# DeltaNet followed by a maxout feed-forward: block products in sets of 32 on 64 rows, weights fetched from ScalarE's queue, TensorE in program order through the first group

## The chip, the cores and the metric

One core of a Trainium2 chip. The metric is the device time of one execution in us. Every kernel was also run in rounds beside the kernel before on the same chip; ratios below come from such rounds. Times within an execution (landmarks, stages, waits) come from one profiled execution of each kernel. Engines: PE is TensorE (PEld its weight loads), DVE VectorE, ACT ScalarE, POOL GpSimd, SP SyncE.

## The reference, cut to what matters

```python
# q, k, v: (4, 8, 768, 48), beta: (4, 8, 768)
k_n = k / (norm(k) + 1e-6)
for t in range(768):
    y[t]  = q[t] @ state
    v_old = k_n[t] @ state
    state = state + beta[t] * outer(k_n[t], v[t] - v_old)
x = y as (3072 tokens, 384)
h = maximum(maximum(x @ w1, x @ w2), x @ w3)      # w1, w2, w3: 384 x 768
out = h @ w_out                                   # 768 x 384
```

## The kernel before

The sequence is cut into 12 chunks of 64 tokens. A chunk needs the inverse of a triangular 64x64 matrix for each of 32 (batch, head) pairs. It is built from smaller blocks: VectorE solves the diagonal blocks row by row (`solve`), and TensorE joins them. For the first two groups (chunks 0 to 3) VectorE solves blocks of 16, joined to 32 (`halves_z`, `halves_u`, tiles p_e and p_f, called e and f below) and then to 64 (`join_z`, `join_u`, tiles p_z and p_j: z and j); for later groups it solves blocks of 32. With the inverse `ut`, the chain of a chunk goes on: `new` (p_u), `step` (p_s, the state), `to_y` (p_y), `to_x` (p_x, transposed for the feed-forward). `ffn(m)` then runs the maxout layer of 512 tokens (p_h, p_o). The attention work of group m+1 is spread between the maxout items of group m; only group 0 has nothing to hide behind. That opening, and group 0's maxout, are what the change rearranges.

```python
    def fetch():                       # one weight piece, 384 KB
        ...
            st = work.tile([128, 2 * 384], U32, name="w_bits", bufs=4)
            nc.sync.dma_start(out=..., in_=src)

    TILES = [(bb, g) for bb in range(2) for g in range(2)]
    # rows(bb): 64 rows, half bb;  block(bb, f): 32 rows, half f of half bb

    def halves_z(c):                   # e: 64 products of 32 rows, 16 columns
        ...
        for g in range(2):
            for h in range(H):
                for bb in range(2):
                    for f in range(2):
                        r = block(bb, f)
                        nc.tensor.matmul(p_v[r, g, h],
                            at[g][r, h, BL * f : BL * (f + 1)], d[r, g, h, HB:])

    def new(c):                        # u, for comparison
        for h in range(H):
            for bb, g in TILES:
                nc.tensor.matmul(p_v[rows(bb ^ g), g, h],
                    ut[c % NU][rows(bb), g, h], rhs[rows(bb), g, h])

    # the opening, all engines in program order:
    ...; halves_z(0); halves_u(0); halves_z(1); join_z(0); ...; halves_u(1)
    join_u(0); ...; join_z(1); ...; new(0); ...; join_u(1); ...; to_y(0); to_x(0)
    # then ffn(0), ordered by the scheduler, with the links of chunks 1 to 3 between
```

A product in float32 is two instructions (two passes), each with its weight load; so a set of 32 products is 64 TensorE instructions in the tables.

## Time and profile before

| | |
|---|---|
| time before, first three runs | 615.88 us median |
| TensorE idle until the first p_h (76.1 us), between there and 160, after 160 | 32.5, 14.7, 8.2 us |
| clock at half in 43 to 76 | all of it |
| TensorE instructions | 8794 matmuls, as many weight loads |

The views behind this table, and how they are read, stand in the prediction.

### The profile page before, as it was taken

The page shows a single profiled execution, that of the slowest core. Times are in us where ns is not written, and L with a number is a line of the kernel's source. Part 1 is how long each engine was busy: PE and PEld are TensorE (multiplying, and loading weights), DVE is VectorE, ACT ScalarE, POOL GpSimd, SP SyncE. Part 2 cuts the span into 40 slices and gives each one's busy share as a digit, 9 for nine tenths or more (in the row PEclk, how much of TensorE's full clock was granted, in tenths as well). Part 3 has the DMA queues.
Part 4 walks back from the last instruction along what each step waited for, and adds up shares of the span by engine and source line. Part 5 has one row for each costly group of instructions (what it writes and reads, how often), then busy time and mean ns, then how long its engine had stood idle before and what let it go on. Part 6 is the DMA issues. An engine that isn't in the chain of part 4 may idle for free.

```text
span 614.8 us, 19609 instructions
## 1 busy us (share of the span) xinstructions
PE 559.4 (91%) x8794; PEld 342.7 (56%) x8794; DVE 304.8 (50%) x713; ACT 160.8 (26%) x292; POOL 77.4 (13%) x108
## 2 busy tenths in 40 slices
PE   6644667978999999999999999999999999999996
PEld 5534556867655665555655546655556455554443
DVE  1652599328739962389542499432595422101110
ACT  3231545236613142121233121232111111110000
POOL 5360274114400000000000000000000000000000
PEclk9655569897999999999999999999999999999999
DMA  8985257652673254421452321522103100010002
GB/s 156 178 203 123 73 137 141 137 145 70 125 123 65 48 121 74 87 49 31 90 105 58 63 54 27 108 54 61 21 14 82 28 2 3 13 39 1 0 1 52
DMA packets 140820, 45.46 MB, mean 74 GB/s; under 512 B 126400, under 2 KB 136384, under 8 KB 140736
## 3 DMA queue, kind: packets, MB, share of 16 engines
q1 hardware_dynamic: 137744, 41.45, 33.2%
q0 software_dynamic: 880, 2.36, 1.4%
q8 instruction: 69, 1.13, 0.8%
q10 hardware_dynamic: 2112, 0.39, 0.4%
q14 instruction: 15, 0.12, 0.1%
HBM read 29.98 MB, written 14.16 MB: 72 GB/s over the span
## 4 chain that ended last, share of the span: by engine, by line
PE 70%; DVE 16%; issue 5%; POOL 3%; DMA 2%; SPq 2%; ACT 1%; POOLq 0%; ACTq 0%; DVEq 0%
PE p_h L707 37%; PE p_o L731 15%; DVE y_bl L453 4%; DVE tmp L449 4%; PE p_g L356 3%; PE p_t L334 3%; PE p_k L597 2%; DVE h L717 1%; PE p_q L597 1%; PE p_y L660 1%; PE p_z L564 1%; SPq L112 1%; PE p_s L643 1%; PE p_u L625 1%; PE p_e L521 1%
## 5 line engine op out<-in xcount | busy, mean ns | idle before, releaser
L707 PE MATMUL p_h<-xt,w_sb 128*128 128x512 f32 (+1 forms) x702 | 301.3, 575 | 2.0 <-DVE xt L693 1.3
L707 PEld LDWEIGHTS p_h<-xt,w_sb 128*128 128x128 f32 x702 | 130.9, 195 | 124.8 <-issue 116.6
L717 DVE TENSOR_TENSOR h<-h,p_h 128x512 f32<-128x512 f32 (+1 forms) x78 | 50.2, 644 | 142.9 <-PE p_h L707 142.8
L731 PE MATMUL p_o<-wo_sb,h 128*128 128x384 f32 x288 | 97.1, 490 | 2.5 <-DVE h L717 2.4
L731 PEld LDWEIGHTS p_o<-wo_sb,h 128*128 128x128 f32 x288 | 53.3, 190 | 41.3 <-DVE h L717 6.5
L453 DVE TENSOR_TENSOR y_bl<-y_bl,tmp 128x31 f32<-128x31 f32 (+20 forms) x154 | 52.7, 342 | 4.2
L449 DVE TENSOR_TENSOR tmp<-x_bl,y_bl 128x31 f32<-128x31 f32 (+20 forms) x154 | 51.8, 337 | 4.2
L715 ACT COPY h<-p_h 128x512 f32<-128x512 f32 (+1 forms) x39 | 21.5, 551 | 122.1 <-PE p_h L707 122.1
L356 PE MATMUL p_g<-kqt 64*64 64x64 f32 (+1 forms) x1280 | 32.1, 249 | 11.0 <-ACT kqt L340 10.5
L275 POOL TENSOR_TENSOR v_t<-v_t,nrm 128x768 f32<-128x768 f32 x12 | 18.2, 1513 | 180.7 <-DMA v_t<-in_v_dram 93.7
L356 PEld LDWEIGHTS p_g<-kqt 64*64 64x64 f32 x1280 | 27.6, 149 | 18.1 <-ACT kqt L340 14.0
L739 ACT COPY o_sb<-p_o 128x384 f32<-128x384 f32 x24 | 11.5, 480 | 88.3 <-PE p_o L731 85.3
L340 ACT COPY kqt<-p_t 128x512 f32<-128x512 f32 (+1 forms) x32 | 25.2, 797 | 31.2 <-PE p_t L334 31.0
L509 DVE STREAM_TRANSPOSE t<-ut 32x256 f32<-32x256 f32 x32 | 13.9, 434 | 23.1 <-DMA ut<-y_d 22.8
L236 POOL TENSOR_TENSOR w_sb<-mant,up 128x384 int32<-128x384 int32 x18 | 18.7, 1036 | 20.6 <-DVE mant L232 11.6
L334 PE MATMUL p_t<-ident,kpad 128*128 128x128 f32 x96 | 17.0, 308 | 4.3 <-DVE pt L366 2.1
L366 DVE TENSOR_TENSOR pt<-p_g,mask 128x512 f32<-128x512 f32 x24 | 16.1, 686 | 9.1 <-PE p_g L356 8.8
L374 ACT COPY at<-p_g 128x512 f32<-128x512 f32 x20 | 11.6, 586 | 32.2 <-DVE pt L366 29.7
L213 POOL TENSOR_SCALAR mant<-mant 128x384 f32<-128x384 f32 x24 | 12.7, 531 | 51.9 <-ACT mant L209 51.8
L625 PEld LDWEIGHTS p_u<-v_t,ut 64*64 64x64 f32 x768 | 13.2, 142 | 8.9 <-issue 7.7
L334 PEld LDWEIGHTS p_t<-ident,kpad 128*128 128x128 f32 x96 | 12.5, 156 | 8.8 <-issue 5.5
L643 PEld LDWEIGHTS p_s<-u,kpad 64*64 64x64 f32 x704 | 12.2, 144 | 9.1 <-issue 5.3
(97 smaller groups left out, 503.1 us busy)
## 6 DMA issues: line engine op xcount, KB each, us to landing
w_bits<-in_moe_w_dram SPq DMA_DIRECT2D x18, 384.0 KB, 3.6
at_d<-at SPq DMA_DIRECT2D x36, 128.0 KB, 2.5
qpad<-in_q_dram SPq DMA_DIRECT2D x48, 96.0 KB, 3.1
v_t<-in_v_dram SPq DMA_DIRECT2D x24, 192.0 KB, 4.3
out_dram<-o_sb SPq DMA_DIRECT2D x48, 96.0 KB, 2.2
kpad<-in_k_dram SPq DMA_DIRECT2D x44, 96.0 KB, 3.4
x_bl<-at_d SPq DMA_DIRECT2D x22, 128.0 KB, 3.6
y_d<-y_bl SPq DMA_DIRECT2D x11, 256.0 KB, 3.0
```

The lines of the kernel that those rows point to most:

```text
L236: nc.gpsimd.tensor_tensor(out=dst.bitcast(I32), in0=mant_v.bitcast(I32), in1=up_v, op=ALU.add)
L334: nc.tensor.transpose(p_t[:, i, j * 128 : (j + 1) * 128], src[:, 2 * j : 2 * j + 2], ident,)
L340: nc.scalar.copy(kqt.rearrange("p j b i t -> p i (j b) t")[:, some], p_t.rearrange("p i (x t) -> p i x t", t=C)[:, some],)
L356: nc.tensor.matmul(p_g[rows(bb ^ (g * i)), par, c0 : c0 + C * (1 + whole)], kq[:, 0], kq if whole else kq[:, i],)
L449: nc.vector.tensor_tensor(out=t_v, in0=row.to_broadcast(t_v.shape), in1=column.to_broadcast(t_v.shape), op=ALU.mult,)
L453: nc.vector.tensor_tensor(out=rest, in0=rest, in1=t_v, op=ALU.subtract)
L597: nc.tensor.matmul(p_b[rows(bb), par, c0 : c0 + D], kqt[g][rows(par), j, bb ^ g, i], st[rows(par), bb ^ g, g, j],)
L625: nc.tensor.matmul(p_v[rows(bb ^ g), g, h], ut[c % NU][rows(bb), g, h], rhs[rows(bb), g, h],)
L707: nc.tensor.matmul(p_h, w_sb[i][:, t, f * 128 : (f + 1) * 128], xt[:, t, lo : lo + w], start=(t == 0), stop=(t == KT - 1),)
L715: nc.scalar.copy(h, p_h)
L717: nc.vector.tensor_tensor(out=h, in0=h, in1=p_h, op=ALU.max)
L731: nc.tensor.matmul(p_o, hs[f][:, i * 128 : (i + 1) * 128], wo_sb[:, f], start=(f == 0), stop=(f == FT - 1),)
```

## The change

The intent: fewer TensorE instructions and steps before the first p_h; weight fetches that no longer block SyncE's queue; and TensorE's order in group 0 fixed by hand. Its core (left out: the same edits for the links' tables, loads and warm-up):

```diff
-    def fetch():
+    def fetch(queue=nc.scalar):
...
+        for h in range(H):                                  # halves_z
+            for bb, g in TILES:
+                r = rows(bb)
+                nc.tensor.matmul(
+                    p_v[r, g, h], at[g][r, h], second[r, g, h, :, 1]
+                )
+        nc.scalar.copy(zs[c % NU], p_v)
+        fine[c] = [square("t") for g in range(2)]
         for g in range(2):
-            for h in range(H):
-                for bb in range(2):
-                    for f in range(2):
-                        r = block(bb, f)
-                        nc.tensor.matmul(...)
...
+        for h in range(H):                                  # halves_u
+            for bb, g in TILES:
+                r = rows(bb)
+                nc.tensor.matmul(p_v[r, g, h], t[g][r, h], z[r, g, h])
+        (four scaled copies of the corners into ut; the copies of fill() are gone)
...
-        queues = (nc.gpsimd, nc.sync) if m == 0 else one_queue  # end of solve
...
-                    to = dg[cc] if m < FINE else ut[cc][:, :, :, BL * half :]
-                    queues[half].dma_start(
+                    nc.sync.dma_start(          # solved blocks, straight into ut
...
-    load_beta()                                             # the opening
+    load_beta()            # later, and in GpSimd's queue
+    blocks(0, two_queues)  # x_bl: two transfers on SyncE, two on GpSimd
+    sums_0 = first_squares()
...
+    first_norms(*sums_0)
+    for n in range(2):
+        fetch(nc.sync)     # two weight pieces directly behind x_bl
     load_k(6)
...
-    halves_z(1)            # chunk 1 leaves the opening
...
+    FIRST = { 0: "s0 e1 T2", 1: "k1 f1 P2 T3", 2: "z1 P3", 3: "q1 j1", 4: "u1 T4", ...
+    by_hand.enter_context(tc.manual_schedule(engines={mybir.EngineType.PE}))
+    for i, _ in enumerate(ffn(0)):
...
-        nc.gpsimd.memset(y_bl, 0.0)
+        (nc.vector if m else nc.gpsimd).memset(y_bl, 0.0)
```

More of the change, by code (lines that the diff above doesn't have):

```diff
@@ L140, in load_beta @@
             half, cc = divmod(i, 2)
-            nc.sync.dma_start(
+            nc.gpsimd.dma_start(
                 out=beta_bl[32 * i : 32 * (i + 1)],
@@ L161 @@
     ut = [const.tile([128, 2, H, C], FP32, name=f"ut{i}") for i in range(NU)]
-    dg = [const.tile([128, 2, H, BL], FP32, name=f"dg{i}") for i in range(NU)]
     t1 = [const.tile([128, 2, H, BL], FP32, name=f"t1{i}") for i in range(NU)]
@@ L189, in fetch @@
             st = work.tile([128, 2 * 384], U32, name="w_bits", bufs=4)
-            nc.sync.dma_start(
+            queue.dma_start(
                 out=st.rearrange("p (a b) -> p a b", a=a), in_=src
@@ L464, in solve @@
         for cc in range(2):
-            for half in (1, 0):
+            for half in range(2):
                 for bb in range(2):
                     r0 = C * bb + BL * half
-                    to = dg[cc] if m < FINE else ut[cc][:, :, :, BL * half :]
-                    queues[half].dma_start(
-                        out=to[r0 : r0 + BL].rearrange("p g h i -> p (g h) i")[
-                            :, :, 0:BL
-                        ],
+                    nc.sync.dma_start(
+                        out=ut[cc][
+                            r0 : r0 + BL, :, :, BL * half : BL * (half + 1)
+                        ].rearrange("p g h i -> p (g h) i"),
                         in_=y_d[half, cc, 2 * bb : 2 * bb + 2].rearrange(
@@ L498, in block @@
         return slice(C * bb + BL * f, C * bb + BL * f + n)
-    def parts_of(c):
-        if c < 2 * FINE:
-            return [dg[c % NU]] * 2
-        return [ut[c % NU][:, :, :, BL * f : BL * (f + 1)] for f in range(2)]
     def turn_t1(c):
-        first, t = parts_of(c)[0], t1[c % NU]
         for bb, g in TILES:
-            nc.vector.transpose(out=t[block(bb ^ g), g], in_=first[block(bb), g])
+            nc.vector.transpose(
+                out=t1[c % NU][block(bb ^ g), g], in_=ut[c % NU][block(bb), g, :, 0:BL]
+            )
@@ L511, in halves_z @@
+    fine = {}
     def halves_z(c):
         at = [ats[2 * c + g] for g in range(2)]
-        d, t, z = dg[c % NU], t1[c % NU], zs[c % NU]
+        u_t = ut[c % NU]
+        second = u_t.rearrange("p g h (f two x) -> p g h f two x", two=2, x=HB)
         p_e = ps_two("p_e")
-        p_v = by_head(p_e, HB)
-        for g in range(2):
-            for h in range(H):
-                for bb in range(2):
-                    for f in range(2):
-                        r = block(bb, f)
-                        nc.tensor.matmul(
-                            p_v[r, g, h],
-                            at[g][r, h, BL * f : BL * (f + 1)],
-                            d[r, g, h, HB:],
-                        )
@@ L526, in halves_z @@
-        nc.scalar.copy(z[:, :, :, 0:HB], p_v)
-        nc.vector.transpose(
-            out=t.rearrange("p g h x -> p (g h x)"),
-            in_=d.rearrange("p g h x -> p (g h x)"),
-        )
+        p_v = by_head(p_e, BL)
+        for h in range(H):
[3 more added lines that the diff above has]
+                    p_v[r, g, h], at[g][r, h], second[r, g, h, :, 1]
+                )
+        nc.scalar.copy(zs[c % NU], p_v)
+        fine[c] = [square("t") for g in range(2)]
@@ L532, in halves_u @@
+        for g in range(2):
+            nc.vector.transpose(
+                out=fine[c][g].rearrange("p h x -> p (h x)"),
+                in_=u_t[:, g].rearrange("p h x -> p (h x)"),
+            )
     def halves_u(c):
-        d, t, z = dg[c % NU], t1[c % NU], zs[c % NU]
+        t, z = fine.pop(c), zs[c % NU]
         p_f = ps_two("p_f")
-        p_v = by_head(p_f, HB)
-        for g in range(2):
-            for h in range(H):
-                for bb in range(2):
-                    for f in range(2):
-                        r = block(bb, f, HB)
-                        nc.tensor.matmul(
-                            p_v[block(bb, f), g, h], t[r, g, h], z[r, g, h, 0:HB]
-                        )
@@ L544, in halves_u @@
-        corner = d[:, :, :, HB:]
-        nc.vector.tensor_tensor(out=corner, in0=corner, in1=p_v, op=ALU.subtract)
-        turn_t1(c)
-    def fill(c):
-        for bb in range(2):
-            for f in range(2):
-                r = block(bb, f)
-                nc.scalar.copy(
-                    ut[c % NU][r, :, :, BL * f : BL * (f + 1)], dg[c % NU][r]
-                )
+        p_v = by_head(p_f, BL)
+        for h in range(H):
+            for bb, g in TILES:
+                r = rows(bb)
+                nc.tensor.matmul(p_v[r, g, h], t[g][r, h], z[r, g, h])
@@ L556, in join_z @@
+        for f in (1, 0):
+            for bb in range(2):
+                r = block(bb, f, HB)
+                to = ut[c % NU][r, :, :, BL * f + HB : BL * (f + 1)]
+                of = p_v[r, :, :, HB * f : HB * (f + 1)]
+                if bb:
+                    nc.vector.tensor_scalar_mul(to, of, -1.0)
+                else:
+                    nc.scalar.mul(to, of, -1.0)
+        turn_t1(c)
     def join_z(c):
         at = [ats.pop(2 * c + g) for g in range(2)]
-        z, second = zs[c % NU], parts_of(c)[1]
+        z, second = zs[c % NU], ut[c % NU][:, :, :, BL:C]
@@ L568, in join_z @@
         nc.vector.tensor_copy(z[block(1)], p_v[block(1)])
-        if c < 2 * FINE:
-            fill(c)
     def join_u(c):
@@ L631, in new @@
         copied(c, u, p_v)
+        if c + NU < 2 * FINE:
+            for bb in range(2):
+                nc.vector.memset(ut[c % NU][block(bb), :, :, BL:C], 0.0)
     def step(c):
@@ L757, with busy @@
     nc.scalar.sqrt(warm, warm)
-    load_beta()
     load_k(4)
     load_k(5)
-    def busy(n, w=128):
+    def busy(n):
         p_w = ps_ffn([128, TOK], "p_w")
@@ L767 @@
     two_queues = (nc.sync, nc.gpsimd)
-    busy(8)
+    busy(6)
     for n in (0, 1):
@@ L774 @@
             turn(n + 2, (0,))
+    load_beta()
+    blocks(0, two_queues)
+    sums_0 = first_squares()
+    turn(4, (0,))
+    turn(5, (0,))
+    first_norms(*sums_0)
+    for n in range(2):
+        fetch(nc.sync)
     load_k(6)
     load_k(7)
-    blocks(0, two_queues)
-    turn(4, (0,))
-    turn(5, (0,))
-    first_norms(*first_squares())
     for n in range(3):
         load_q(n)
-    load_v(0)
-    for _ in range(4):
-        fetch()
     some(solving, 1)
@@ L788 @@
         gram(n, (0,), (nc.gpsimd, nc.gpsimd))
+    load_v(0)
+    for n in range(2):
+        fetch(nc.sync)
     some(solving, HB - 1)
     some(solving, 1)
-    scale(0, nrm_0[:, 0])
-    busy(16)
+    busy(12)
     for n in range(2):
@@ L797 @@
     some(solving, 2)
-    load_q(3)
-    load_q(4)
+    scale(0, nrm_0[:, 0])
     for n in (6, 7):
@@ L803 @@
     blocks(1)
+    halves_z(0)
+    load_q(3)
+    load_q(4)
     some(conv, 1)
-    halves_z(0)
     halves_u(0)
-    halves_z(1)
     join_z(0)
+    fetch()
     some(conv, 1)
-    halves_u(1)
     join_u(0)
     fetch()
-    fetch()
-    join_z(1)
     old_k(0)
@@ L817 @@
     new(0)
+    some(conv, 1)
     load_v(1)
+    to_y(0)
     fetch()
+    some(conv, 1)
+    to_x(0)
     fetch()
-    join_u(1)
-    some(conv, 1)
-    to_y(0)
-    to_x(0)
-    some(conv, 1)
-    scale(1, nrm_0[:, 1])
     load_v(2)
@@ L829 @@
     tc.no_sync_barrier()
+    scale(1, nrm_0[:, 1])
     solving = solve(1)
-    some(solving, 1)
     LINKS = {
@@ L846 @@
     FIRST = {
-        0: "s0", 1: "k1 q1", 3: "u1", 4: "y1", 5: "s1", 6: "x1",
+        0: "s0 e1 T2", 1: "k1 f1 P2 T3", 2: "z1 P3", 3: "q1 j1", 4: "u1 T4",
+        5: "y1 T5", 6: "s1 P4", 7: "x1 T6", 8: "P5 T7", 12: "P6", 14: "P7",
     }
@@ L852 @@
     )
-    BY_UNIT = dict(t=turn, g=gram)
+    BY_UNIT = dict(
+        t=turn, g=gram, T=lambda n: turn(n, (1,)), P=lambda n: gram(n, (1,))
+    )
     SOLVE = 12
@@ L860, in links @@
                 BY_CHUNK[f](2 * m + i)
-            if f in BY_UNIT and m + 1 < GROUPS:
-                BY_UNIT[f](4 * (m + 1) + i)
-    for m in range(GROUPS):
-        shift = 0 if m else 9
-        for i, _ in enumerate(ffn(m)):
-            if m == 0:
-                some(conv, 1)
-                fetch()
-                if i in (0, 1):
-                    n = 2 + i
-                    turn(n, (1,))
-                    gram(n, (1,))
-                    load_q(n + 3)
-                links(0, FIRST.get(i, ""))
-                if 4 <= i < 8:
-                    turn(i, (1,))
-                    gram(i, (1,))
-                    if i == 4:
-                        load_q(7)
-                        load_v(3)
-                if i == 8:
-                    prep(2)
-                    prep(3)
-                links(1, EARLY_LINKS.get(i, ""))
-                if i < shift:
-                    some(solving, 3)
-            i -= shift
-            for group, first in ((m + 3, 18), (2, -4 if m == 0 else 99)):
-                if group < GROUPS and first <= i < first + 4:
-                    n = 4 * group + i - first
-                    load_k(n)
-                    if n % 4 < 3:
-                        load_q(n)
@@ new lines, in links @@
+            if f in "TP":
+                BY_UNIT[f](i)
+                if f == "T" and i + 3 < 11:
+                    load_q(i + 3)
+            elif f in BY_UNIT and m + 1 < GROUPS:
+                BY_UNIT[f](4 * (m + 1) + i)
+    by_hand = ExitStack()
+    by_hand.enter_context(tc.manual_schedule(engines={mybir.EngineType.PE}))
+    for i, _ in enumerate(ffn(0)):
+        some(conv, 1)
+        fetch()
+        links(0, FIRST.get(i, ""))
+        links(1, EARLY_LINKS.get(i, ""))
+        if 2 <= i < 9:
+            some(solving, 3)
+        if i == 4:
+            load_v(3)
+        if 5 <= i < 9:
+            load_k(3 + i)
+        if i == 8:
+            prep(2)
+            prep(3)
+        if i == 12:
+            load_q(11)
+        if i in (15, 18):
+            load_v(4 + i // 18)
+        if i in (18, 20):
+            prep(4 + i // 20)
+        if i == 19:
+            blocks(2)
+        if i == 21:
+            solving = solve(2)
+            some(solving, 1)
+        if i >= 21:
+            some(solving, 4)
+        if i >= 27:
+            load_k(i - 15)
+            if i < 30:
+                load_q(i - 15)
@@ L895 @@
+    some(solving, 40)
+    by_hand.close()
+    for m in range(1, GROUPS):
+        for i, _ in enumerate(ffn(m)):
+            if m + 3 < GROUPS and 18 <= i < 22:
+                n = 4 * (m + 3) + i - 18
+                load_k(n)
+                if n % 4 < 3:
+                    load_q(n)
             if m + 2 < GROUPS:
@@ L909 @@
                     some(solving, 4)
-            if m:
-                links(m + 1, LINKS.get(i, ""))
+            links(m + 1, LINKS.get(i, ""))
         some(solving, 40)
```

## The prediction

> **What bounds the kernel now.** I read the page's forty slices first. Each digit is a tenth of busy time; PEclk is the granted TensorE clock.
>
> ```profile
> PE   6644667978999999999999999999999999999996
> ...
> PEclk9655569897999999999999999999999999999999
> ```
>
> From slice 11 on, TensorE is full at the full clock; before that it is neither. So there are two kernels here: a tail in which only the amount of TensorE work counts, and an opening in which a chain of small steps counts. Then I cut the span into stages: until the first block product, until the first maxout matmul, until the first half of group 0's maxout, and so on.
>
> ```profile
> 43.00:76.00 33.00, 18.20 (x902) 16.25 (x902) 12.37 (x24) 11.91 (x23) 6.30 (x11) 0.50 0.48 107
> 76.00:118.00 42.00, 32.95 (x660) 26.65 (x661) 33.91 (x80) 18.00 (x38) 20.57 (x24) 0.82 0.65 135
> 118.00:160.00 42.00, 36.33 (x1053) 29.63 (x1052) 21.50 (x50) 22.09 (x42) 12.32 (x15) 0.84 0.55 133
> 160.00:210.00 50.00, 49.53 (x750) 28.60 (x749) 37.33 (x90) 13.13 (x29) 6.99 (x7) 1.00 0.45 81
> 210.00:614.80 404.80, 397.06 (x5023) 219.79 (x5021) 179.23 (x412) 80.72 (x133) 11.84 (x9) 1.00 0.23 47
> ```
>
> The columns are length, then busy time (and instructions) of PE, PEld, DVE, ACT and POOL, then clock. The last 405 us are TensorE alone; the change touches nothing there but one memset, so whatever it wins must come before 210. In 43 to 76 no engine is half busy except TensorE, and that at half clock: a chain. In 76 to 118 VectorE is the fullest engine for the length (33.9 of 42, or 81%).
>
> What TensorE waits for in 43 to 76 (engine and line waiting, releaser, total us, times, longest):
>
> ```profile
> PE p_z L564 <- issue: 5.9, 2, 3.8
> PE p_f L541 <- issue: 3.2, 2, 1.6
> PE p_e L521 <- DMA dg<-y_d: 2.5, 2, 2.0
> PE p_e L521 <- issue: 2.3, 1, 2.3
> PE p_j L579 <- issue: 0.6, 1, 0.6
> ```
>
> "issue" means no semaphore explains the wait: 12.0 us together. In the timeline these gaps come every 122 to 127 matmuls, that is every 250 instructions with their weight loads (two waits of 1.65 and 2.25 us stand at 46 and 50, one of 3.80 at 54). The queue table has an entry of just that period:
>
> ```profile
> q8 instruction: 69, 1.13, 0.8%
> ```
>
> 1.13 MB in 69 packets is 16 KB each; 2 x 8794 TensorE instructions over 69 is 255 per packet. So TensorE runs out of instructions when it eats small products faster than blocks of 255 arrive.
>
> **What the Trainium skill says.** "Runtime: NRT & Kernel Launch", section Instruction fetch mechanics: instructions stream in blocks of 16 KiB, 256 instructions, and crossing a boundary is mostly hidden. The period agrees with the trace (255); "hidden" does not here: 12.0 us in 33. "TensorE: Matmul & The Clock Gate", section LDWEIGHTS: the load time goes with the columns, not the rows. The groups of 43 to 72 agree in sense: 64 matmuls of 64 columns (p_u) take 2.0 us, 256 of 32 columns (p_e) take 4.3 us, so about 31 against 16 ns each. Same page, Part 1: the clock is half or full, by recent activity; the trace grants 0.50 in the whole of 43 to 76. "DMA: Bandwidth & Descriptors", section Issuing engines are not separate DMA queues: another issuing engine saves only issue time. This trace adds that an issuer also stops at a wait: SyncE stood 44.9 us before weight fetches.
>
> ```profile
> SPq L190 <- DVE mant L232: 44.9, 11, 11.2
> ```
>
> **The change, part by part.**
>
> *Smaller blocks.* The two products that build a 32-block from 16-blocks, per chunk, were 64 products each (128 instructions in two passes) on 16 or 32 rows. They become 32 on 64 rows (64 instructions), for 4 chunks: 4 x 2 x 64 = 512 matmuls fewer, and 12 fewer warm-up ones: 8794 becomes about 8270. In TensorE time this is nothing: 128 x 16 = 2.0 us before, 64 x 31 = 2.0 us after, cold; 128 x 10 = 1.3 against 64 x 17 = 1.1 us warm (p_y: 64 in 1.08). What falls is instructions: the 512 matmuls with their loads are 4 blocks of 255. Around them: the four copies that filled ut (0.61 us each on ScalarE, 2.45 a chunk) and the subtraction (0.42, VectorE) go; two scaled copies per engine (some 0.4 each, from the 0.36 to 0.42 of the old one) and a second transpose of 128x512 (0.71) come. VectorE: about +1.1 us a chunk; ScalarE about -1.4.
>
> *Chunk 1 leaves the opening.* Its block products, joins and fills went between those of chunk 0; now they stand among the first four maxout items. Of the 902 matmuls of 43 to 76, the chain keeps six sets of 64 (e, f, z, j, u, y) and 6 transposes, 390.
>
> *The solved blocks go straight into ut, all from SyncE.* The GpSimd half was issued only at 39.9, behind GpSimd's own work, against 37.5 on SyncE. Issued from SyncE alone, four of 0.48 us from about 37, landing some 2.5 us later: 41.5 instead of 43.7. That saves about 2 us. The earlier beta, k and x_bl order I count as 0 to 0.5.
>
> *The chain of chunk 0*, from 41.7 (durations of before, cold): e 2.1, z copy 0.7, f 2.1, corners 0.9, z products 1.2, its copies behind the four transposes (4 x 0.43) 1.6, j 1.2, its copies 0.8 and a conversion's VectorE work 0.9 at worst, u 2.1, copies 1.2, y 2.1, copies 1.3, x 1.6, copies 1.2: 21.0 us with 0.1 a hop. I allow no more: 780 instructions are 3 blocks over 20 us, so fetches mostly hide. The first maxout matmul: about 62.5 instead of 76.1, 13.5 us earlier.
>
> *The first maxout half (76 to 118 before, 42 us).* VectorE's 33.9 us grow by chunk 1's work (2 x 0.71 + 2 x 0.4 + 1.74 + 0.69 + 0.69 = 5.3), the memset of y_bl that moves from GpSimd (about 1) and ut's clearing (0.4): 40.6. At 93% busy, as at its densest now, 43.5 us. So this half ends near 106 instead of 118: 1.5 us are given back.
>
> *Chunks 2 and 3 and the rest of group 0 (118 to 210).* Idle in 118 to 160 is 5.7 us, 3.8 of it "issue" between 131 and 138; a clock of 0.84 means a third of 42 us at half speed, and the busy two thirds of that cost about 4.5 more. Half the instructions and a planned order should save half of these 10 us; gram products of two units that slip in from the first half cost 1.2. Net 4 us, so group 0 ends near 194, some 16 earlier.
>
> *Weights on ScalarE.* SyncE's 44.9 us of standing no longer holds up q loads and at_d behind it. ScalarE pays about 0.6 us for each of 20 fetches, in a stage where it is 43% busy. I count zero, as enabling the rest.
>
> *Tail.* Four memsets of 0.6 to 1 us on VectorE where it is full around 275 and 370 (TensorE idle 1 to 1.4 us there): +0.5 to +1 us in all.
>
> Sum: -2 - 11.5 + 1.5 - 4 + 0.7 = -15.3; 615.9 becomes 600.6, say **600**.
>
> **The rivals.** (1) *VectorE becomes the bound of 62 to 106 more than I think*: all that left the opening meets weight conversion, solve(1) and masks there. VectorE operations stretch when GpSimd runs (a 32-wide operation of 0.2 us took 0.97 to 1.1). Then the first half takes 48 us and the gain is 10: 606. (2) *Program order on TensorE stalls*: one late ScalarE or VectorE copy stops all behind it, and the clock halves. Before, one such wait was 5.2 us (p_g for kqt, whose copy stood behind conversion work on ScalarE). ScalarE now also holds fetches that may wait. Three such waits take 8 us: 608. Against it: the order is placed by hand with one or two items of slack. (3) *The fetch stalls stay*, because they come from DMA crowding and not from instruction counts: then the opening wins only 8 and the time is 606. Against it: their period of 250 instructions. (4) *Better*: with chunks 0 to 3 free of stalls the clock stays full from 66 on, and all 14 us of loss in 76 to 118 (9 idle, about 5 cold) shrink: 590.
>
> **Range and chances.** 2% faster is below 603.6. My sum lies 3.5 us inside, the rivals 1 to 3 lie 2 to 5 outside, one lies well inside. I give 589 to 611 for eight in ten; faster 0.64, within 2% 0.33, slower 0.03, as nothing in the 405 us tail is at stake.
>
> **What would show it.** The first p_h near 62.5; "issue" waits of TensorE before it down from 12 to under 4 us; about 8270 matmuls and 65 instruction packets; the four stretches e, f of chunks 2, 3 without gaps over 1 us; VectorE over 90% busy from 62 to 106; group 0's last p_o near 194; the rest of the span still about 405 us. Wrong it would be if p_h starts after 68, if TensorE waits for ScalarE or VectorE more than 12 us between p_h's start and its 60th matmul, or if the stretch after group 0 grows by more than 3 us.

## The result, and the profile after

The changed kernel takes 612.16 us (median of 4; before 616.43 on the same chip), 0.9929 of before, 95% interval 0.9907 to 0.9951: faster by 0.7%, which counts as the same at 2%, and just outside the predicted range of 589 to 611. A ratio is the mean time of one kernel's fast runs over that of the other's of the same rounds, so not quite the ratio of the medians quoted.

The forty slices of the kernel after, busy tenths of TensorE and the granted clock:

```profile
PE   5547884998999999999999999999999999999997
...
PEclk9755578999999999999999999999999999999999
```

The full stretch begins where it did, at slice 11; only the second half of group 0 (slices 8 to 10) has lost its cold spots. The stages of the kernel after, cut at its own landmarks (first whole set of e, first p_h, 54th p_h instruction, and so on; columns as before):

```profile
0.00:45.60 45.60, 24.16 (x404) 20.25 (x404) 19.94 (x58) 13.67 (x27) 20.28 (x46) 0.75 0.85 165
45.60:68.70 23.10, 16.32 (x386) 14.44 (x386) 11.43 (x24) 7.54 (x16) 5.78 (x8) 0.50 0.57 128
68.70:118.00 49.30, 38.44 (x848) 32.36 (x848) 43.67 (x98) 23.98 (x50) 22.65 (x30) 0.81 0.74 171
118.00:160.00 42.00, 38.20 (x1002) 31.51 (x992) 29.07 (x69) 19.28 (x39) 11.53 (x13) 1.00 0.48 101
160.00:206.00 46.00, 46.00 (x627) 26.51 (x620) 33.57 (x90) 9.80 (x19) 3.04 (x2) 1.00 0.37 66
206.00:611.20 405.20, 397.55 (x5024) 220.28 (x5023) 177.35 (x396) 80.81 (x133) 7.46 (x5) 1.00 0.23 47
```

Two things are to be seen. From its first whole set to the first p_h the chain takes 23.1 us instead of 32.3, but that set starts at 45.7: before it was 43.7, and the prediction had 41.7. And the first maxout half takes 48.7 us instead of 42.2, so that at its end the change stands where the kernel before stood. Landmarks, from each kernel's timeline, against the prediction:

| us from the start | before | predicted | after |
|---|---|---|---|
| solve(0) starts | 22.6 | 22.1 to 22.6 | 24.8 |
| first p_h | 76.1 | 62.5 | 68.8 |
| 54th p_h instruction ends | 118.3 | 106 | 117.5 |
| last p_o of group 0 ends | 210.7 | 194 | 207.3 |
| rest of the span | 404.2 | 404.8 | 403.9 |

The fetch stalls did go from the chain. That they are fetches, the traces support further: before, the six "issue" waits of TensorE between 43 and 76 end at its recorded instructions 1217, 1474, 1730, 1985, 2241 and 2498 (in order of start, loads counted), 255 to 257 apart, and a packet of q8 starts within 1.3 us of the start of each of the first five (at 46.3, 50.3, 56.0, 59.8 and 63.8 us). After, the waits in 45.6 to 68.7 are copies, but for one of 0.4 us for a transfer, and none is "issue" (the longest three below); in the first maxout half 3.1 us of "issue" remain (p_k 2.0, p_q 1.1).

```profile
PE p_j L566 <- DVE z L557: 1.3, 1, 1.3
PE p_u L612 <- ACT ut L568: 0.8, 1, 0.8
PE p_j L566 <- ACT z L556: 0.7, 1, 0.7
```

But the timeline of the chain shows the sets themselves (start, length, engine, line, operation, shapes, count, wait before it):

```profile
45.67 3.59 PE L515 MATMUL p_e<-ut,at 64*64 64x32 f32 x60 [0.35 <-DMA ut<-y_d]
...
49.93 3.65 PE L533 MATMUL p_f<-z,t 64*64 64x32 f32 x64 [0.68 <-ACT z L518]
...
60.41 1.94 PE L612 MATMUL p_u<-v_t,ut 64*64 64x48 f32 x60 [0.18 <-DVE ut L569]
...
63.52 1.95 PE L650 MATMUL p_y<-u,pt 64*64 64x48 f32 x62 [0.15 <-DVE u L683]
```

(The p_u line and the p_y line are at the same half clock.) Sets of e and f take nearly twice as long as sets of u and y, with the same weights (64x64) and fewer moving columns (32 against 48). I had priced them like u. That became the first question; the second was why the solve began later, and the third what filled the first maxout half.

### The profile page after: what moved, and what is told of

Its sections match the earlier page's. It is cut to its first block, busy times and chain, and to the rows that moved or that the text cites. A ratio compares the mean times of both kernels' runs of the same rounds, so it can differ in the third digit from the quotient of the medians.

```text
span 611.2 us, 18549 instructions
## 1 busy us (share of the span) xinstructions
PE 560.7 (92%) x8270; PEld 345.4 (57%) x8270; DVE 315.0 (52%) x730; ACT 155.1 (25%) x284; POOL 70.7 (12%) x102
## 3 DMA queue, kind: packets, MB, share of 16 engines
q8 instruction: 65, 1.06, 0.7%
## 4 chain that ended last, share of the span: by engine, by line
PE 71%; DVE 15%; DMA 6%; issue 3%; SPq 2%; ACT 1%; POOL 1%; POOLq 0%; ACTq 0%; DVEq 0%
PE p_h L697 39%; PE p_o L721 16%; DMA w_bits<-in_moe_w_dram 3%; DVE y_bl L452 3%; DVE tmp L448 3%; PE p_g L355 3%; PE p_t L333 3%; PE p_k L584 2%; PE p_u L612 2%; PE p_y L650 2%; PE p_q L584 1%; DVE h L707 1%; PE p_j L566 1%; PE p_e L515 1%; DVE t L499 1%
## 5 line engine op out<-in xcount | busy, mean ns | idle before, releaser
L697 PE MATMUL p_h<-xt,w_sb 128*128 128x512 f32 (+1 forms) x702 | 297.9, 571 | 1.8 <-DVE xt L683 1.2
L452 DVE TENSOR_TENSOR y_bl<-y_bl,tmp 128x31 f32<-128x31 f32 (+20 forms) x154 | 54.0, 351 | 4.1
L499 DVE STREAM_TRANSPOSE t<-ut 32x256 f32<-32x256 f32 x48 | 20.7, 432 | 6.0 <-DMA ut<-y_d 5.2
L612 PE MATMUL p_u<-v_t,ut 64*64 64x48 f32 x768 | 16.1, 234 | 7.3 <-DVE ut L569 4.5
L333 PE MATMUL p_t<-ident,qpad 128*128 128x128 f32 x96 | 16.7, 301 | 6.1 <-DMA qpad<-in_q_dram 5.7
L208 ACT ACTIVATE mant<-w_bits 128x384 f32<-128x384 f32 x24 | 13.3, 556 | 22.3 <-DMA w_bits<-in_moe_w_dram 11.8
```

Source lines behind the costliest of these rows:

```text
L333: nc.tensor.transpose(p_t[:, i, j * 128 : (j + 1) * 128], src[:, 2 * j : 2 * j + 2], ident,)
L452: nc.vector.tensor_tensor(out=rest, in0=rest, in1=t_v, op=ALU.subtract)
L499: nc.vector.transpose(out=t1[c % NU][block(bb ^ g), g], in_=ut[c % NU][block(bb), g, :, 0:BL])
L612: nc.tensor.matmul(p_v[rows(bb ^ g), g, h], ut[c % NU][rows(bb), g, h], rhs[rows(bb), g, h],)
L697: nc.tensor.matmul(p_h, w_sb[i][:, t, f * 128 : (f + 1) * 128], xt[:, t, lo : lo + w], start=(t == 0), stop=(t == KT - 1),)
```

## The experiments

All are the changed kernel with the edit shown, five rounds each. Three chips were used for the first twelve, four to a chip, and a fourth for the last.

**Control: the changed kernel again.**

> Control: the changed kernel itself, on the chip of the runs beside it. About 0.993 of the kernel before, as at first; the earlier four variants ran on another chip than the changed kernel had. If it is nearer 0.990 here, the 0.9898 of the alternating order was the chip and not the edit.

Measured: 612.65 us, 0.9933 (0.9904 to 0.9963); solve(0) at 23.8, first p_h at 67.9, 54th p_h at 117.1. The result stands. The 0.9898 of the alternating order (next) came from another chip; its interval overlaps the control's, so these runs do not tell whether that edit won 2 us in some other way, or the chip differs. A difference of 0.3% between ratios of two chips proves nothing here.

**Alternating halves.**

```diff
-            for bb, g in TILES:      # in halves_z and halves_u
+            for g, bb in TILES:
```

> Only the order of the 32 products of a set in e and f changes: row halves alternate, where the changed kernel puts two products in a row on the same half of rows and columns. Theory A (a product whose weights go to the same 64x64 quarter as the one before can't overlap its load): a set of 64 instructions falls from 3.6 us cold and 2.08 us warm to about 1.9 and 1.1, as for p_u; first p_h 68.8 becomes about 65.6; the time falls by 4 to 8 us, to 604 to 608. Rival (the width of 32 columns or the strided operand is what is slow): the sets keep 3.6 and 2.08 us and the time stays at 612.

Measured: 611.59 us, 0.9898 (0.9879 to 0.9917). The f set of the opening, in this kernel's timeline:

```profile
49.36 3.62 PE L533 MATMUL p_f<-z,t 64*64 64x32 f32 x64 [0.68 <-ACT z L518]
```

3.62 us against 3.65: the order of the products does nothing to the length of a set. Theory A falls, as far as it spoke of neighbours in the order.

**Four quarters.** In the changed kernel a product takes its rows from half bb and puts its columns in half bb too, so a set touches only the two 64x64 quarters on the array's diagonal. p_u puts odd g across (`rows(bb ^ g)`) and uses all four. The edit does the same for e and f; VectorE's transpose for odd g then swaps the halves, in two instructions instead of one.

```diff
-                    p_v[r, g, h], at[g][r, h], second[r, g, h, :, 1]
+                    p_v[rows(bb ^ g), g, h], at[g][r, h], second[r, g, h, :, 1]
...
-                r = rows(bb)
-                nc.tensor.matmul(p_v[r, g, h], t[g][r, h], z[r, g, h])
+                r = rows(bb ^ g)
+                nc.tensor.matmul(p_v[rows(bb), g, h], t[g][r, h], z[r, g, h])
...
+        for bb in range(2):
+            nc.vector.transpose(out=fine[c][1][rows(1 - bb)]..., in_=u_t[rows(bb), 1]...)
```

> Products of e and f with odd g are put across: rows of one half, columns of the other, so that a set uses all four 64x64 quarters of the array, as p_u does, instead of the two on the diagonal. Theory A2 (each quarter takes one load and one pass at a time, so the rate goes with how many quarters a set uses, and their order does not matter): sets fall from 3.35 to about 1.9 us cold and from 1.84 to about 1.1 us warm, first p_h 3 us earlier, TensorE busy less by 6 to 9 us, time 3 to 8 us below the control. Rival (32 columns, or a stationary operand of 64 columns with so few moving ones, is slow by itself): sets stay at 3.35 and 1.84 us, time as the control.

Measured: 607.82 us, 0.9851 (0.9827 to 0.9876), against the control's 0.9933 on the same chip: 4.8 us. The result is correct. Its sets:

```profile
48.30 1.92 PE L515 MATMUL p_e<-ut,at 64*64 64x32 f32 x60 [0.71 <-DMA ut<-y_d]
...
50.89 1.93 PE L537 MATMUL p_f<-z,t 64*64 64x32 f32 x64 [0.68 <-ACT z L518]
```

and the groups of the whole span (busy time, mean ns), first of the changed kernel, then of this run:

```profile
L533 PE MATMUL p_f<-z,t 64*64 64x32 f32 x256 | 11.6, 255 | 0.7 <-ACT z L518 0.7
L515 PE MATMUL p_e<-ut,at 64*64 64x32 f32 x256 | 10.5, 238 | 1.6 <-DMA ut<-y_d 1.6
```

```profile
L537 PE MATMUL p_f<-z,t 64*64 64x32 f32 x256 | 5.9, 247 | 1.4 <-DVE v_t L600 0.7 <-ACT z L518 0.7
L515 PE MATMUL p_e<-ut,at 64*64 64x32 f32 x256 | 5.8, 237 | 2.8 <-DMA ut<-y_d 1.9 <-ACT kqt L339 0.9
```

The time of one instruction is nearly the same (237 and 247 ns against 238 and 255); what halves is the distance between starts. From first to last start, an f set of the opening takes 3.35 us in the changed kernel, 3.33 with alternating halves, and 1.64 with four quarters. Over 63 steps that is 53 and 26 ns; times the two and four quarters, 106 and 104 ns. So each quarter takes one load and pass per about 105 ns at half clock, in both orders that were tried.

The single starts of that set show the same: with alternating halves two come within 7 ns and the next after 100, with four quarters four come within 20 ns and the next after 87, so 107 ns a turn in both. The old sets of e, on 32x32 blocks, had four starts within 20 ns and the next after 34: a turn of 54 ns with half as many weight columns. So the prediction's step from 16 to 31 ns fits; it holds for four blocks or quarters at work, and the new sets used two. The rival (few columns, or wide weights, are slow by themselves) is out: the shapes did not change.

From the first product of e to the first p_h the chain takes 20.9 us (24.2 in the control); counted from the first whole set, as the prediction counts, 19.7 (23.1), where it had 20.8. The first maxout half takes 44.2 instead of 49.2 (predicted 43.5). That chunk 1's sets, and what waits behind them, made part of that half slow is likely but not shown: a kernel without this edit also came to 44.1 there (weights on SyncE, below).

This run's solve(0) started at 27.2 in the profile, which is of its slowest execution (609.6 us), so the second cause shows even in it.

**Weights behind the loads.**

```diff
-    for n in range(2):
-        fetch(nc.sync)
     load_k(6)
     ...
+    for n in range(2):
+        fetch(nc.sync)
```

> The first two weight fetches are issued after the k and q loads instead of directly behind x_bl. Theory B (768 KB of weights crowd the two x_bl transfers that GpSimd issues, 7.8 us to landing against 4.9 before): solve(0) starts at about 22.5 instead of 24.75 and everything up to the first p_h shifts by 2 us; the time falls by 0 to 2 us, as far as the first maxout half passes it on. Rival (it is beta in GpSimd's queue, or k and q, that delays): start of solve(0) stays at 24 to 25.

Measured: 610.64 us, 0.9886 (0.9865 to 0.9907); solve(0) at 23.6, between the two theories' numbers. The eight profiles with x_bl and the first weights as changed, the changed kernel and its control among them, give 23.8 to 24.9 and once 27.2, so one profile can't carry a difference of 1 us. The time is that of the alternating order on the same chip (0.9898). x_bl from GpSimd's queue still takes 6.4 us to land.

**x_bl from SyncE, weights behind the loads.**

```diff
-    blocks(0, two_queues)
+    blocks(0)                 # all four transfers of x_bl on SyncE
```

> The changed kernel with all four x_bl transfers of the first solve issued by SyncE (two were GpSimd's) and the first weights behind the q loads. Theory B2 (GpSimd's two transfers land 7.5 us after their issue because its queue also holds beta, and because 768 KB of weights run beside them): solve(0) starts near 20 instead of 23.8 to 24.9, first p_h near 64 instead of 68, and the time falls 2 to 4 us against the changed kernel (0.993 of before becomes 0.987 to 0.990). Rival (all DMA engines are full then, whoever issues): solve(0) stays after 22.5.

Measured: 608.19 us, 0.9862 (0.9842 to 0.9882); solve(0) at 20.9, first p_h at 64.8. x_bl's transfers between 12 and 27 us (count, size, median us from issue to landing), first of the control, then of this run:

```profile
x_bl<-at_d SPq DMA_DIRECT2D x2, 128.0 KB, 3.5
x_bl<-at_d POOLq DMA_DIRECT2D x2, 128.0 KB, 7.0
```

```profile
x_bl<-at_d SPq DMA_DIRECT2D x4, 128.0 KB, 3.4
```

The same 128 KB take twice as long from GpSimd's queue, and were issued there later (15.0 and 15.8 us, against 13.2 and 13.6 on SyncE). The rival, that full DMA engines delay x_bl whoever issues it, falls. Of B2, that the queue decides is tested by the next run; why GpSimd's is slow here is not shown. Before the change, with beta not in that queue, the same transfers landed in 4.9 us (3.6 from SyncE), and in the run with late weights, beta still ahead of them, in 6.4. So beta ahead of them is the likelier reason, but no run moves beta alone.

**x_bl from SyncE alone, with four quarters.** The weights are back directly behind x_bl.

> The both-run with the first weights back directly behind x_bl: only the issuing engine of x_bl(0) and the quarters differ from the changed kernel. With weights late but x_bl on GpSimd, solve(0) started at 23.6; with both, at 20.5 to 22.5. If the issuing engine is what counts, it starts at 20.5 to 22 here and the time is within 1.5 us of the both-run (0.978 of before); if the place of the weights is needed as well, it starts at 22.5 or later and the time is 2 us or more above (0.981 or more).

Measured: 603.73 us, 0.9798 (0.9775 to 0.9821); solve(0) at 22.0, x_bl landing in 3.2 us. This lies at the edge of the first of the two expectations (20.5 to 22; by the ratios 1.3 us above the both-run, which comes next), so the issuing engine is the main cause. What the place of the weights is worth, some 1 us, neither this run nor the one with late weights can prove.

**Both corrections together.**

> The x_bl change together with the four quarters. If the two causes are independent, they add up: first p_h near 61 to 62, which is where the prediction put it, and the time near 604 to 605 (0.978 to 0.981 of before). If VectorE in the first maxout half takes it back, the first p_h comes early all the same, but the time stays at 0.984 or above.

Measured: 602.84 us, 0.9777 (0.9755 to 0.9799), correct; faster than both kernels, and the only one that is faster than before by 2% beyond its interval. First p_h at 61.3, 54th p_h at 106.0, last p_o of group 0 at 197.7. The two causes add up within the noise: against the control's ratio, four quarters gave 0.8%, x_bl with its weights 0.7%, both 1.6% (x_bl and both ran on another chip than the control). Its slices and stages:

```profile
PE   6656778889999999999999999999999999999997
...
PEclk9655778899999999999999999999999999999999
```

```profile
41.40:61.30 19.90, 13.10 (x391) 11.19 (x391) 12.43 (x25) 7.55 (x16) 5.86 (x8) 0.50 0.71 149
61.30:106.00 44.70, 35.74 (x820) 29.25 (x824) 41.23 (x95) 22.84 (x48) 22.38 (x27) 0.81 0.83 177
```

The chain takes 19.9 us and the first half 44.7, with VectorE 92% busy in it.

**A shorter solve.** Its output is wrong, which doesn't matter for the time.

```diff
+            if m == 1 and j >= 2:
+                yield
+                continue
```

> Wrong result on purpose: solve(1) makes 2 of its 15 steps, so VectorE loses 26 operations, some 10 us, between 85 and 116. Theory D (VectorE bounds the first maxout half): from the first to the 54th p_h instruction 48.7 us become about 40, and the time falls by 5 to 9 us. Rival (TensorE's own order, weight transfers or ScalarE bound that half): that stretch stays within 3 us and the time within 3.

Measured: 613.84 us, 0.9936 (0.9914 to 0.9958), so no gain; in its profile the stretch from the first to the 54th p_h took 44.8 us instead of 48.7, VectorE busy for 36.5 of it. But that profile is of the fastest of six executions (609.53 us), so it is no typical one. Taking some 7 us from VectorE gave less than 4 in that stretch, and nothing in the time. That VectorE alone bounds the half and the time with it is refuted. Runs that leave VectorE's work in that stretch as it was, and e and f on two quarters, spread as widely (44.1 to 49.2), so the 4 us are not shown to be the edit's either.

**TensorE ordered by the scheduler.**

```diff
-    by_hand.enter_context(tc.manual_schedule(engines={mybir.EngineType.PE}))
```

> TensorE's program order in group 0 is given up: the scheduler orders it, as before the change; all else as changed. If program order costs stalls (the 6.3 us wait of p_u at 99 to 103.6), the time falls by 2 to 5 us; if program order is what keeps the chain of chunk 1 and the 16-blocks early, it rises by 3 to 10 us. I hold a rise for likelier.

Measured: 616.58 us, 0.9978 (0.9957 to 0.9999): 0.45% above the control's ratio and 0.8% above the alternating order's, which ran on the same chip: some 3 to 5 us. Both guesses were half right. The 54th p_h ends earlier, at 113.7 instead of 117.5 (no more than that stretch varies between runs); but the 108th ends later, at 157.8 instead of 153.8, with 10.2 us of that second stretch at half clock, where program order has none. So program order is worth its place through chunks 2 and 3, and without it the rest of the change is worth 0.2%.

**Weights on SyncE again.**

```diff
-    def fetch(queue=nc.scalar):
+    def fetch(queue=nc.sync):
```

> Weight fetches go back to SyncE's queue, all else as changed. If taking them off SyncE mattered, loads of q and k stand behind waits for weight buffers again, TensorE waits for p_t or p_g in the first half and the time rises by 2 to 5 us; if not, it is within 1.5 us of the control. I expect a small rise.

Measured: 612.94 us, 0.9929 (0.9903 to 0.9954), as the control. The queue's waits came back in part (18.6 us for weight buffers). I had expected a small rise; there is none to be seen. In its one profile the first maxout half is shorter, 44.1 us against the control's 49.2, but from there to the last p_o of group 0 it takes 92.6 instead of 89.7, and in the time nothing is left: what one stretch wins, the next can give back.

**Fillers**, alone and on top of both corrections: idle TensorE time before the first p_h is filled with unread products.

```diff
+    busy(10)                  # and busy(1) to busy(5) after each set of the chain
```

> Idle TensorE time from 33 us to the first p_h is filled with warm-up products whose result nobody reads. Theory E (the opening chain is slow because the clock stands at half through it: all 24 us between the first e and the first p_h): the clock turns full at about 40 to 45, the six sets of the chain take 1.1 to 1.9 us instead of 1.9 to 3.6, first p_h at 61 to 64 instead of 68.8, time 3 to 7 us below the control if the next half passes it on. Rival (the chain is made of the copies between the sets): first p_h moves by less than 2 us or gets later by the fillers.

> The same with warm-up products in the idle time of TensorE before the first p_h. With sets of 1.7 us cold the chain is copies more than products: if the clock turns full, the six sets shrink by some 4 us together and first p_h comes 2 to 3 us earlier than in the run without fillers; if the fillers only fill, it comes within 1 us of it and the time is the same.

Measured: alone 613.43 us, 0.9916 (0.9879 to 0.9953), first p_h at 66.0, the chain still at half clock for 17 of 23 us: no gain to be told from the control. With both corrections the clock does turn full (half clock for 3.4 us of the chain) and the sets of e and f take 0.92 and 1.06 us, yet the chain shrinks only from 19.9 to 18.2 us, and the time is 607.68, 0.985 (0.9828 to 0.9872), 5 us worse than without fillers. The first p_h comes at 61.9, no earlier, since solve(0) began at 22.5 in this profile (of its slowest execution) and not at 20.5. In its first half p_k waits 5.4 us for VectorE's update of the state:

```profile
PE p_k L588 <- DVE st L643: 5.4, 1, 5.4
```

So the chain is copies more than products, as the rival said. Why the first half then got longer by 4 us is left open; the scheduler may order VectorE differently once TensorE's estimated times shift, but no run shows it.

**VectorE in program order too**, on top of both corrections.

```diff
-    manual_schedule(engines={mybir.EngineType.PE})
+    manual_schedule(engines={mybir.EngineType.PE, mybir.EngineType.DVE})
```

> The same as the both-run, with VectorE too in program order through the first maxout group. Theory F (in the first maxout half the copies of chunk 1's chain stand behind solve(1) and weight conversions on VectorE, as the 7 us between the end of j and VectorE's half of its copy in the changed kernel): the stretch from first to 54th p_h instruction falls from about 44 to 49 to below 42 and the time by 2 to 5 us against the both-run. Rival (program order lets VectorE wait for late operands): stretch and time grow by 2 to 6 us.

Measured: 625.22 us, 1.0131 (1.0109 to 1.0154). The first half took 41.3 us, as theory F had it; then VectorE stood 10.0 us at a stretch for ScalarE (a square root of the norms of later chunks), and TensorE behind it:

```profile
PE p_h L701 <- DVE h L711: 12.7, 1, 12.7
```

## Why the prediction was wrong

The forecast was 600, the time 612.2. By a sign that it named itself it was wrong: the first p_h came after 68, at 68.8. Its frame held: two regions, a chain in the opening, and a tail of 404 us that the change hardly touches. The stretches of the span, in us, with the corrected kernel (both corrections) beside them:

| stretch | before | predicted | after | corrected |
|---|---|---|---|---|
| start to solve(0) | 22.6 | 22.1 to 22.6 | 24.8 | 20.5 |
| solve(0) to the first whole set of e | 21.1 | about 19.3 | 20.9 | 21.0 |
| from there to the first p_h | 32.3 | 20.8 | 23.1 | 19.8 |
| first maxout half | 42.2 | 43.5 | 48.7 | 44.7 |
| from there to the last p_o of group 0 | 92.4 | 88 | 89.8 | 91.7 |
| rest | 404.2 | 404.8 | 403.9 | 403.6 |

Its own steps, one by one:

- **"In TensorE time this is nothing" failed.** The prediction priced the new sets of e and f at 31 ns an instruction cold and 17 warm, as measured on p_u and p_y. They took 53 between starts cold (3.35 us over 63), and 29 warm (1.84 us over 63). What it carried over was the shape of the weights; what it did not look at was which quarters of the array a set uses, though the index `rows(bb ^ g)` in `new` and `rows(bb)` in the new code say it. Shown by the run with four quarters: same shapes, same count, rates of 26 cold and about 15 warm, 4.8 us of time. Sized wrong were thus two sets in the chain, some 1.6 us each, and six warm or half-warm sets later, of about 1 us each, with what waits behind them.
- **"The earlier beta, k and x_bl order I count as 0 to 0.5" failed.** It was to be a small gain; solve(0) started 2.1 us later than before (24.75 against 22.62, one profile), and in the other runs with this part 1.2 to 4.6 later. Two of x_bl's transfers stayed in GpSimd's queue, now behind four of beta, and took 7 us to land where SyncE's take 3.5. Shown, as far as the queue goes, by the two runs that issue them from SyncE (solve(0) at 20.9 and 22.0; the first, which also moves the weights, is 4.5 us faster than the control). I had read the 4.9 us of that row before the change, and added nothing for what the new order puts around it. The statement that another issuing engine saves only issue time, which the prediction quotes, did not hold for these transfers.
- **"That saves about 2 us" (solved blocks, all from SyncE) failed too, and the corrected kernel hides it.** From solve(0) to the first whole set of e it takes 20.9 us against 21.1 before; in the other runs, without those that have fillers or VectorE in program order, 20.7 to 21.3. The four transfers of chunk 0 were to be issued in 4 x 0.48 us. But in all these runs one of the four took 1.1 to 1.7 us to issue (1.61 in the changed kernel), and the solve itself took 12.2 us in the changed kernel instead of 11.9. With fillers alone no issue is long, and the step takes 19.5 us. Why one issue is long is open. SyncE's lines, before (GpSimd issued the other four, from 39.9) and after, both with chunk 1's transfers:

```profile
37.52 1.93 SPq L469 DMA_DIRECT2D dg<-y_d  x4
```

```profile
40.10 5.33 SPq L465 DMA_DIRECT2D ut<-y_d  x8
```

- **The chain's sum was about right.** With four quarters it took 19.7 to 19.8 us from the first whole set, predicted 20.8 (the items listed add up to 21.0 before any hop). Fetch stalls hid, as said: no "issue" wait in it, 65 packets, 8270 matmuls.
- **The first maxout half**, 43.5 predicted, took 48.7, so it gave back 6.5 us of the gain and not 1.5; with four quarters 44.2, 44.7 and 43.8, but 48.6 with fillers. So its length fits the sets as I priced them, as far as single profiles tell; but what bounds it is not shown. VectorE's share there was 87 to 94%, its work 43.7 us where 40.6 were predicted; yet taking 7 us from it moved the time by nothing. The program-order wait of rival 2 exists, in the timeline of the changed kernel: p_j ends at 95.4, ScalarE's half of the copy comes at 98.3, VectorE's at 102.9, and p_u waits.

```profile
98.25 0.58 ACT L568 ACTIVATE ut<-p_j 32x512 f32<-32x512 f32 x1
...
102.85 0.69 DVE L569 TENSOR_SCALAR ut<-p_j 32x512 f32<-32x512 f32 x1
103.59 1.05 PEld L612 LDWEIGHTS p_u<-v_t,ut 64*64 64x64 f32 x36 [4.46 <-DVE ut L569]
```

- **Chunks 2 and 3 and the rest of group 0**: from the 54th p_h to the last p_o 89.8 us, predicted 88, before 92.4. Right in sign and nearly in size; the run without program order takes 97.5 us for the same stretch, so it is that part of the change which brings it, with the clock full.
- **Weights on ScalarE count zero**: right for the time, shown by the run that takes them back.

With the first two terms mended the kernel takes 602.84, the first p_h comes at 61.3 (62.5), the 54th ends at 106.0 (106) and group 0 at 197.7 (194). That is 9.6 us by the ratios against before (0.9933 and 0.9777), of 12 that were missing. But that the landmarks now meet the prediction is in part luck: x_bl from SyncE starts solve(0) 2.1 us earlier than before, which the prediction did not have, and that makes up for the 2 us of the third term, which did not come. What remains lies in the second half of group 0 and is not settled, nor is what bounds the first half.

## What to carry to other kernels

When small products are packed into the array, write down for each set which row half and column half every product uses, and count the distinct quarters: that count set the rate here, not the order in the two orders tried, and not the number of instructions. When the start of a chain hangs on one small transfer, give it to the queue that lands it soonest and look at what is queued before it. A rate carried over from a neighbouring row of the profile is only as good as the likeness of what the two rows do, so check the placement as well as the shape. And when a corrected kernel meets the forecast, compare it stretch by stretch: two errors can cancel, as they do here before the first whole set of e.

## What the Trainium skill lacked or had wrong

- "TensorE: Matmul & The Clock Gate", Part 3, says that a weight load overlaps matmuls in flight only when its row group differs. Here that isn't what decided the rate: sets with alternating row halves on two quarters ran at 53 ns a start (cold), as without alternation, while sets over all four quarters, in which every second pair of neighbours shares a row half, ran at 26. "TensorEngine Tiling (Array Packing)", Available Configurations, has the four 64x64 tiles, but not what products on the same one cost: about 105 ns per load and pass at half clock, about 58 at full.
- "Runtime: NRT & Kernel Launch", Instruction fetch mechanics, holds fetches for mostly hidden. Before the change, TensorE stood at every 256th instruction or so among small products, 12.0 us in 33; in the chain after it not at all, in the half behind it 3.1 us.
- "DMA: Bandwidth & Descriptors", Issuing engine by pattern, calls the hardware queues generally faster; the page has no size for a whole transfer amid other traffic. Here 128 KB landed in 3.5 us from SyncE and 7.0 from GpSimd in the same 15 us of one run, and in 3.6 and 4.9 before the change, so the difference depends on what else runs.
- No page has what filling idle TensorE time is worth when the chain is copies: full clock in all but 3.4 us of the chain won 1.7 us of 19.9 there, and the whole kernel lost 5.
